# A Fourier-mixing layer beside a ReLU MLP on one Trainium2 core: the opening stretch re-ordered, twelve x tiles transposed by DMA

## Chip, core and metric

One NeuronCore of a Trainium2 chip. Five engines have queues of their own that run in order: PE (TensorE, matmuls and weight loads), DVE (VectorE), ACT (ScalarE), POOL (GpSimd) and SP (SyncE, which here only issues DMAs). Sixteen DMA engines move the data. Matmul results land in PSUM; everything else lives in SBUF or in HBM. The metric is the device time of one launch in microseconds (us); lower is better.

## What is computed

x is 2048 x 576, w1 576 x 4608, w2 4608 x 576, all float32.

```python
xn = _layernorm(x, axis=-1)
a = xn @ dft_hid_re.T ;  b = xn @ dft_hid_im.T
A = dft_seq_re @ a - dft_seq_im @ b
B = relu(xn @ w1) @ w2
return x + A + B
```

(The einsums of the reference are written as matrix products here.)

## The kernel before

**Arithmetic.** Each float32 operand is split into two float16 parts, `hi` and `lo`, after a scaling by a power of two, and each product is three float16 matmuls. Products on w2, and most others, are done as seven block products instead of eight (the `PRODUCTS` list, numbered 0 to 6), so that sums of blocks (`S1..S4` of the activations, `T1..T4` of w2) are built first, on DVE.

**Stages.** x is cut into 16 tiles of 128 rows and 4 groups of 4 tiles (tiles 0 to 3, 4 to 7, 8 to 11, 12 to 15). The hidden dimension of the MLP is cut into 9 blocks of 512 columns. A step is a pair (block, group): `mlp1` makes relu(xn w1) of it, `mlp1_out` evicts it from PSUM (ACT writes the hi parts, DVE the lo parts and the sums), and one step later `mlp2` multiplies it by w2. The 36 steps run from the start to about 815 us; the DFT along the hidden dimension and then the one along the sequence follow. The change touches the opening stretch (the first 62 us or so), and what it moves reaches to about 120 us.

**How a tile of x is made ready.** `stats` (L197) takes mean and variance of a group on DVE (`bn_stats`, `bn_aggr`), one square root on ACT (L215), and six small DVE instructions. `normalize` (N, L242) writes the normalised tile in float32 on DVE (L247) and its float16 high part on ACT (L249), into one of four staging buffers (`dbufs`, tile number modulo 4). `remainder` (E, L251) subtracts the two for the low part, on POOL in the opening stretch and on DVE later. Then the tile is transposed into `xT`: either by ten PE transposes into PSUM and two ACT copies out of it (`transposes`, T, L268; tiles 0 to 7), or by two DMA transposes on SP's queue (`transposes_dma`, TD, L260; tiles 8 to 15): nine blocks of 128 columns, and the last 128 columns once more for the half-filled block.

**The opening stretch** (L747 to L864) is written out by hand. Loads of x, w1 and w2 go out on SP, then sixteen copies of x from HBM to the HBM buffers `spill` (L760), to which POOL's accumulating DMAs (L573) later add the MLP's output. Four tiles of group 0 and then group 1 are transposed and multiplied by w1 block 0 (`tile_by`, then `mlp1` on whole groups). Meanwhile w2's scale is worked out: ACT sums magnitudes (`sum_w2`, L646), PE and DVE find the largest (`power_pe`, L152), and `split_w2` and `sums_w2` make the float16 parts. The steps of `prepare_w2(0)` are a list `w`: `w[0]`, `w[1]` sum magnitudes, `w[3]` makes the scale, `w[4]`/`w[6]` split the four plain blocks of the two halves, `w[5]`/`w[7]` make the sums, the rest split the sums. The stretch ends with products 0 to 2 on w2, the first two `mlp1` results of group 2 (`early`), and products 3 to 6.

**What sets the order.** A planner puts each engine's instructions into a queue: in program order where an instruction is ready by its own estimate of times, else behind others that are ready. `tc.issue_after(i)` (and `behind(key)`, which looks an instruction up in the dictionary `order`) makes what is traced inside it follow `i` on `i`'s own engine; on other engines it does nothing. Waits between engines are put in by the framework from the data.

**After the opening stretch** comes the loop over steps (L963). Its first pass, `n == 2`, does group 2 of block 0 and makes tiles 12 to 15 ready (N, E on DVE, TD). `work()` takes the next item of `todo`, which prepares the weights of the coming block: `load_w1`, `max_w1`, `split_w1`, `load_w2`, `sum_w2`, and so on; their raw loads share two buffers.

Of the kernel before, what the change touches and what calls it, by code (L numbers as in the profile page):

```python
# [49 lines left out]
def kernel(  # L50
# [47 lines left out]
    def load_raw(key, src, shape):  # L98
        r = raws[key] = raw.tile(shape, F32, tag="raw", name="raw_" + "_".join(map(str, key)))
        nc.sync.dma_start(r, src)  # L100
# [8 lines left out]
    def load_w2(b, i):  # L109
        load_raw(("w2", b, i), w2[b, i], [P, 4, EH])  # L110

# [40 lines left out]
    def power_pe(s, p, m):  # L152

        n = m.shape[-1]
        ps = ps2.tile([P, 2, 512], F32, tag="ps2", name="pm")

        for c in range(n):
            nc.tensor.matmul(
                ps[:1, 0, c * P : (c + 1) * P], m[:, c : c + 1], ident.bitcast(BF16),
                start=True, stop=True,  # L160
            )
        top = small.tile([1, n], BF16, tag=f"top{n}", name="top")
        nc.vector.tensor_reduce(
            top, ps[:1, 0, : n * P].rearrange("p (n f) -> p n f", f=P), AX.X, ALU.max
        )
        nc.tensor.matmul(ps[:, 1, :n], ones, top, start=True, stop=True)
        half = small.tile([P, n], F32, tag=f"half{n}", name="half")
        nc.vector.tensor_scalar(half, ps[:, 1, :n], 2.0**-107, 2.0**6, ALU.max, ALU.mult)
# [11 lines left out]
    def split(hi, lo, src, s):  # L180

        nc.scalar.activation(hi, src, AF.Copy, scale=s)  # L182
        nc.vector.scalar_tensor_tensor(lo, src, s, hi, ALU.mult, ALU.subtract)  # L183
# [13 lines left out]
    def stats(ts, after=None):  # L197
# [9 lines left out]
        for i, st in enumerate(sts):  # L207
            nc.vector.bn_aggr(mv[:, i], st.rearrange("p a b -> p (a b)"))
            yield
# [32 lines left out]
    def normalize(t, eng=nc.vector, after=None):  # L242
        stage = dbufs[t % 4]
        xn = xns[t] = stage[:, :D]

        xs = xss[t] = stage[:, D : 2 * D].bitcast(F16)
        eng.tensor_scalar(xn, acc[t], means[t], factors[t], ALU.subtract, ALU.mult)  # L247
        with behind(after):
            nc.scalar.activation(xs[:, :D], acc[t], AF.Identity, bias=shifts[t], scale=factors[t])  # L249

    def remainder(t, eng):  # L251
        xn, xs = xns[t], xss[t]
        eng.tensor_tensor(
            xs[:, D : D + REM], xn[:, KM * P :], xs[:, KM * P : D], ALU.subtract
        )
        eng.tensor_tensor(
            xs[:, D + REM :], xn[:, : KM * P], xs[:, : KM * P], ALU.subtract
        )

    def transposes_dma(t):  # L260

        xs = xss[t]
        g, c = divmod(t, TG)
        dst = xT[g][:, :, c * P : (c + 1) * P]
        nc.sync.dma_start_transpose(dst[:, :NKX], xs)
        nc.sync.dma_start_transpose(dst[:, NKX], xs[:, D - P : D])

    def transposes(t):  # L268
        xs = xss[t]
        pt = ps2.tile([P, 2, 1024], F16, tag="ps2", name=f"pt{t}")  # L270
        for k in range(NKX):
            nc.tensor.transpose(
                pt[:, k // 8, (k % 8) * P : (k % 8 + 1) * P], xs[:, k * P : (k + 1) * P], ident
            )
        g, c = divmod(t, TG)

        nc.tensor.transpose(pt[:, 1, P : 2 * P], xs[:, D - P : D], ident)
        dst = xT[g][:, :, c * P : (c + 1) * P]
        nc.scalar.activation(
            dst[:, :8, :], pt[:, 0, :].rearrange("p (k t) -> p k t", t=P), AF.Copy  # L280
        )
        order["xT", t] = nc.scalar.activation(
            dst[:, 8:, :], pt[:, 1, : 2 * P].rearrange("p (k t) -> p k t", t=P), AF.Copy
        ).ins
# [37 lines left out]
    def mlp1_group(b, g, i, cols, ps, wk=WK, start=True, stop=True):  # L322
        for n, (kx, hl, k) in enumerate(wk):
            nc.tensor.matmul(  # L324
                ps[:, cols], w1s[b, i // 2][:, hl, i % 2 * KT + k], xT[g][:, kx, cols],
                start=(start and n == 0), stop=(stop and n == len(wk) - 1),
            )
# [29 lines left out]
    def mlp1_out(b, g, i, pa, pb, after=None):  # L357
# [8 lines left out]
        for q, src in ((slice(A11, A11 + 1), a11), (slice(A12, A22 + 1), pb)):  # L366
            hi, lo = (h[:, n, q].rearrange("p a b -> p (a b)") for n in range(2))
            with behind(after):
                nc.scalar.activation(hi, src, AF.Relu)
            stt(lo, src, 0.0, hi, ALU.max, ALU.subtract)  # L370
        stt(s3, a11, 0.0, r21, ALU.max, ALU.subtract)
        stt(s1, a22, 0.0, r21, ALU.max, ALU.add)
        stt(s2, a22, 0.0, s3, ALU.max, ALU.subtract)
        stt(s4, a12, 0.0, s2, ALU.max, ALU.subtract)
# [167 lines left out]
    def mlp2(b, g, n):  # L542
# [25 lines left out]
        else:  # L568
            o = sums[row, col]
            add = nc.vector.scalar_tensor_tensor(o, ps, us[b], o, ALU.mult, ALU.add)  # L570
            order["acc"] = order["vfree"] = add.ins
        if n not in (0, 2, 3):
# [4 lines left out]
    def max_w1(b, f):  # L577
# [6 lines left out]
        with behind("vfree" if b >= BB else ("sh", 1) if f > 1 else None):  # L584
# [65 lines left out]
    def power_w2(b):  # L650
# [3 lines left out]
        else:  # L654
            m = small.tile([P, NQ], BF16, tag="mb2", name=f"mb2_{b}")
            with behind(("sh", 8)):
# [29 lines left out]
    def split_w2(b, i, c):  # L686
# [5 lines left out]
        with behind(None if b else ("xT", 7)):  # L692
            split(w[:, 0, q], w[:, 1, q], src, sc["w2", b][:, i : i + 1])
# [64 lines left out]
    for g, row, col in spill:  # L758
        src = x[(g * TG + row * 2) * P : (g * TG + row * 2 + 2) * P, col * EH : (col + 1) * EH]
        nc.sync.dma_start(spill[g, row, col], src.rearrange("(c p) e -> p c e", p=P))  # L760
# [12 lines left out]
    N, E, T, TD = normalize, remainder, transposes, transposes_dma  # L773
# [37 lines left out]
    T(2)  # L811
# [4 lines left out]
    tile_by(1, (3,), ps)  # L816
    T(3)
    weave(stats([4, 5, 6, 7]))
    N(4)
    E(4, GP)  # L820
# [14 lines left out]
    T(6)  # L835
    tile_by(5, (0, 1), qs)
    T(7)
    weave(stats([8, 9, 10, 11], ("sh", 4)))
    N(8, after=("xT", 5))
    E(8, GP)  # L840
    mlp1_out(0, 0, 1, *ps[2:], after=("xT", 6))
    for t in (9, 10, 11):
        N(t, after=("xT", 7))
        E(t, GP)
    tile_by(6, (0, 1), qs)
    w[3]()
    tile_by(7, (0, 1), qs)
    w[4]()
    w[5]()
    mlp1_out(0, 1, 0, *qs)  # L850
    for f in w[6:]:
        f()
    TD(8)
    q2 = [mlp1(0, 1, 2)]
    TD(9)
    q2.append(mlp1(0, 1, 3))
    mlp1_out(0, 1, 1, *q2)
    TD(10)
    TD(11)
# [85 lines left out]
    def first_c(m):  # L945
        n, q = divmod(m, 4)
        f = firsts[m] = mlp.tile([P, HK, P], F32, tag="first", name=f"f{n}_{q}", bufs=1)
        nc.sync.dma_start(f, blocks_c(n)[q])
# [14 lines left out]
    for n in range(2, len(steps)):  # L963
# [46 lines left out]
        for i in range(NF):  # L1010
# [4 lines left out]
            if i % 2:  # L1015
                mlp1_out(b, g, i // 2, *ps[i - 1 : i + 1])
# [3 lines left out]
            if n == 2:  # L1020
# [3 lines left out]
                transposes_dma(t)  # L1024
# [20 lines left out]
        if n == 2:  # L1045
            for q in range(7):
# [231 lines left out]
```

## Time and profile before

| | before |
|---|---|
| time, median of 3 runs | 1257.16 us (1255.46 to 1257.65) |
| time of the profiled execution | 1256.51 us |
| its span in the profile | 1254.7 us |
| PE busy | 1234.3 us (98%) |
| DVE busy | 1008.9 us (80%) |
| ACT busy | 704.8 us (56%) |
| POOL busy | 155.6 us (12%) |
| DMA moved | 158.08 MB, mean 126 GB/s |
| granted PE clock, mean | 0.999 |

The span runs from the first to the last profiled instruction; 1.8 us of the profiled execution's own time lie around it. A row of a timeline gives the start (us from the span's start), the duration, the engine and line, the operation, what is written and read, the number of instructions merged, and in brackets the engine's idle time before it and what ended it. Starts of successive instructions on one engine overlap by some 60 ns, so that start to start is the better price of one. A busy PE is not PE at its peak, so matmuls are best counted by the time from one start to the next.

### The profile page before, as it was taken

To read this page: it belongs to the slowest core of one execution; us is meant where nothing else is said; L and a number is where in the kernel's file an instruction comes from. 1 tells how busy PE (TensorE), PEld (TensorE's weight loads), DVE (VectorE), ACT (ScalarE), POOL (GpSimd) and SP (SyncE) were. 2 spreads that over 40 slices of the span, in tenths; PEclk is the share of its full clock that TensorE was granted. 3 is DMA by queue.
4 is the path that set the end of the run, shared out by engine and by line. 5 is a ranking of instruction groups with operands and counts; after the bars stand their busy time and mean duration, and the time that the engine had idled before them with its cause. 6 is when DMAs were issued, how large, how long until landed. Compare 5 with 4: busy or idle time off the path is not lost.

```text
span 1254.7 us, 25397 instructions
## 1 busy us (share of the span) xinstructions
PE 1234.3 (98%) x10309; PEld 983.5 (78%) x10309; DVE 1008.9 (80%) x1921; ACT 704.8 (56%) x1194; POOL 155.6 (12%) x199
## 2 busy tenths in 40 slices
PE   8799999999999999999999999999999999999998
PEld 7565657888888888888888888877777777777776
DVE  8999997878878778788787878566788878788885
ACT  5756566676666666766767666444453333333332
POOL 1321111212111111212121212100000000000000
PEclk9999999999999999999999999999999999999999
DMA  9576567666567665766576766630053434433420
GB/s 341 131 127 109 97 125 166 110 133 139 132 117 171 122 150 117 137 140 136 117 153 142 145 126 128 113 95 1 1 172 111 144 102 162 124 133 120 141 87 19
DMA packets 75909, 158.08 MB, mean 126 GB/s; under 512 B 17296, under 2 KB 36240, under 8 KB 75792
## 3 DMA queue, kind: packets, MB, share of 16 engines
q1 hardware_dynamic: 53008, 113.99, 28.3%
q0 software_dynamic: 22784, 42.48, 25.4%
q8 instruction: 80, 1.31, 0.4%
q14 instruction: 37, 0.30, 0.1%
HBM read 106.63 MB, written 51.90 MB: 126 GB/s over the span
## 4 chain that ended last, share of the span: by engine, by line
PE 74%; DVE 17%; DMA 4%; ACT 4%; issue 2%; POOL 0%; SPq 0%; DVEq 0%; ACTq 0%; POOLq 0%
PE p L1210 26%; PE p L556 19%; PE bank L479 19%; PE pd L1091 8%; DVE w2s L183 2%; DMA raw_w<-in_w_dram 1%; DMA acc<-in_x_dram 1%; DVE h L370 1%; PE p L324 1%; DVE h L501 1%; DVE h L377 1%; DMA f<-in_cre_dram 1%; ACT f L955 1%; DVE w1buf L183 1%; DVE dbuf L570 1%
## 5 line engine op out<-in xcount | busy, mean ns | idle before, releaser
L556 PE MATMUL p<-w2s,h 128*128 128x288 f16 x3024 | 409.8, 286 | 8.6 <-DVE w2s L183 3.3
L556 PEld LDWEIGHTS <-h 128*128 128x128 f16 x3024 | 295.5, 98 | 85.7 <-issue 9.8
L1210 PE MATMUL p<-R,cs 128*128 128x288 f16 x2688 | 329.4, 286 | 0.0
L1210 PEld LDWEIGHTS <-cs 128*128 128x128 f16 x2688 | 263.0, 98 | 66.3
L182 ACT ACTIVATE cs<-c,sc_c 128x1024 f16<-128x1024 f32 x112 | 125.1, 1144 | 196.8 <-DVE c L1153 72.6
L183 DVE SCALAR_TENSOR_TENSOR cs<-c,sc_c,cs 128x1024 f16<-128x1024 f32 x112 | 141.0, 1282 | 54.4 <-ACT cs L182 54.4
L479 PEld LDWEIGHTS <-w1buf 128*128 128x128 f16 x1600 | 156.5, 98 | 22.8 <-issue 1.7
L479 PEld LDWEIGHTS <-dbuf 128*128 128x128 f16 x1200 | 117.4, 98 | 17.5 <-issue 1.7
L479 PE MATMUL bank<-xT,w1buf 128*128 128x256 f16 x832 | 109.8, 273 | 0.0
L1091 PE MATMUL pd<-dbuf,xT 128*128 128x288 f16 x832 | 103.8, 286 | 0.0
L479 PE MATMUL bank<-acc,w1buf 128*128 128x256 f16 x768 | 102.1, 273 | 1.0 <-DVE acc L509 0.9
L1091 PEld LDWEIGHTS <-xT 128*128 128x128 f16 x832 | 80.8, 98 | 22.0 <-issue 1.9
L501 DVE TENSOR_TENSOR h<-s,h 128x1024 f16<-128x1024 f32 x56 | 68.5, 1223 | 33.9 <-ACT h L498 33.6
L573 POOL DMA_DIRECT2D spill<-dbuf x70 | 60.9, 875 | 233.1 <-DVE dbuf L570 201.9
L486 ACT ACTIVATE h<-acc 128x256 f16<-128x256 f32 x112 | 45.9, 411 | 77.5 <-DVE acc L509 74.8
L479 PE MATMUL bank<-xT,dbuf 128*128 128x256 f16 x624 | 82.4, 273 | 0.0
L498 ACT ACTIVATE h<-s 128x1024 f16<-128x1024 f32 x56 | 59.1, 1056 | 35.9 <-DVE s L493 35.1
L479 PE MATMUL bank<-acc,dbuf 128*128 128x256 f16 x576 | 76.6, 273 | 1.0 <-DVE acc L509 0.9
L1216 DVE SCALAR_TENSOR_TENSOR o<-p,us_c,o 128x288 f32<-128x288 f32 x112 | 57.5, 514 | 12.9 <-PE p L1210 12.3
L955 ACT ACTIVATE f<-f 128x1024 f32<-128x1024 f32 x64 | 66.9, 1046 | 0.6 <-DMA f<-in_cre_dram 0.6
L487 DVE SCALAR_TENSOR_TENSOR h<-acc,h 128x256 f16<-128x256 f32 x112 | 47.2, 422 | 21.0 <-ACT h L486 20.8
L573 POOL DMA_DIRECT2D spill<-sum x42 | 36.3, 865 | 184.9 <-DVE sum L570 159.8
(158 smaller groups left out, 1536.8 us busy)
## 6 DMA issues: line engine op xcount, KB each, us to landing
spill<-dbuf POOLq DMA_DIRECT2D x70, 288.0 KB, 5.2
f<-in_cre_dram SPq DMA_DIRECT2D x32, 512.0 KB, 5.8
f<-in_cim_dram SPq DMA_DIRECT2D x32, 512.0 KB, 5.2
c<-in_cre_dram SPq DMA_DIRECT2D x32, 512.0 KB, 4.1
c<-in_cim_dram SPq DMA_DIRECT2D x32, 512.0 KB, 5.0
spill<-sum POOLq DMA_DIRECT2D x42, 288.0 KB, 4.6
raw_w<-in_w_dram SPq DMA_DIRECT2D x17, 640.0 KB, 6.0
raw_w<-in_w_dram SPq DMA_DIRECT2D x18, 576.0 KB, 4.9
```

Source lines behind the costliest of these rows:

```text
L182: nc.scalar.activation(hi, src, AF.Copy, scale=s)
L183: nc.vector.scalar_tensor_tensor(lo, src, s, hi, ALU.mult, ALU.subtract)
L479: nc.tensor.matmul(ps, l, r, start=first and m == 0, stop=m == len(todo) - 1, skip_group_check=not first,)
L487: stt(lo, src, 0.0, hi, ALU.max, ALU.subtract)
L498: order["s"] = nc.scalar.activation(hi_s, st[:, 1:], AF.Copy).ins
L501: order["lo"] = nc.vector.tensor_tensor(lo_s, st[:, 1:], hi_s, ALU.subtract).ins
L556: order["pe"] = nc.tensor.matmul(ps[:, c], h[:, x, qa, c * P : (c + 1) * P], w[:, y, qb], start=first and i == 0 and j == 0, stop=i == NQ ...
L573: nc.gpsimd.dma_start(spill[g, row, col], o, accum_op=ALU.add)
L955: nc.scalar.activation(f, f, AF.Abs, scale=2.0**-10, accum_out=sums_c[:, n, q : q + 1])
L1091: nc.tensor.matmul(ps[j], xT[g][:, kx, c * P : (c + 1) * P], dsp[j][:, hl, k], start=(t % 2 == 0 and n == 0), stop=(t % 2 == 1 and n == le ...
L1210: nc.tensor.matmul(ps, w[:, a, k], r[:, c, rq], start=first and k == 0 and j == 0, stop=k == HK - 1 and j == 2, skip_group_check=not first,)
L1216: order["o"] = nc.vector.scalar_tensor_tensor(o, ps, us["c"][:, n : n + 1], o, ALU.mult, ALU.add).ins
```

## The change

Tiles 0 to 3 are still transposed on PE; tiles 4 to 7 now go by DMA as 8 to 15 did, and every DMA tile takes one DMA of ten blocks instead of two: the staging buffer is 64 float32 columns longer, and an extra instruction (POOL for tiles 4 to 11, ACT for 12 to 15) first copies the last 128 columns behind the low part. The copies of x to `spill` leave the start of SP's queue: group 0's follow tile 11's DMA, group 1's follow tile 15's, and those of groups 2 and 3 follow the first and second load of block 1's w2. The statistics of tiles 8 to 11, N(7) and w2's scale come ahead of the first eviction; the normalised float32 parts of tiles 10 and 11 go from DVE to ACT; both plain splits of w2 come before any of its sums; and product 0 on w2 comes ahead of the first two results of group 2, products 1 to 6 behind them.

```diff
     def load_raw(key, src, shape):
-        nc.sync.dma_start(r, src)
+        order["raw"] = nc.sync.dma_start(r, src).ins
     def load_w2(b, i):
         load_raw(("w2", b, i), w2[b, i], [P, 4, EH])
+        if b == 1:
+            copy_x(2 + i, "raw")
...
-        xs = xss[t] = stage[:, D : 2 * D].bitcast(F16)
-        eng.tensor_scalar(xn, acc[t], means[t], factors[t], ALU.subtract, ALU.mult)
+        xs = xss[t] = stage[:, D : 2 * D + P // 2].bitcast(F16)
         with behind(after):
+            if eng is nc.scalar:
+                nc.scalar.activation(xn, acc[t], AF.Identity, bias=shifts[t], scale=factors[t])
+            else:
+                eng.tensor_scalar(xn, acc[t], means[t], factors[t], ALU.subtract, ALU.mult)
             nc.scalar.activation(xs[:, :D], acc[t], AF.Identity, bias=shifts[t], scale=factors[t])
...
-        dst = xT[g][:, :, c * P : (c + 1) * P]
-        nc.sync.dma_start_transpose(dst[:, :NKX], xs)
-        nc.sync.dma_start_transpose(dst[:, NKX], xs[:, D - P : D])
+        again = xs[:, 2 * D :], xs[:, D - P : D]
+        if eng is nc.scalar:
+            eng.activation(*again, AF.Copy)
+        else:
+            eng.tensor_copy(*again)
+        with behind("td"):
+            order["td"] = nc.sync.dma_start_transpose(xT[g][:, :, c * P : (c + 1) * P], xs).ins
...
-    for g, row, col in spill:
-        src = x[...]
-        nc.sync.dma_start(spill[g, row, col], src.rearrange("(c p) e -> p c e", p=P))
+    def copy_x(g, key="td"):
+        for row, col in itertools.product(range(2), range(2)):
+            t = g * TG + row * 2
+            src = x[t * P : (t + 2) * P, col * EH : (col + 1) * EH]
+            with behind(key):
+                nc.sync.dma_start(spill[g, row, col], src.rearrange("(c p) e -> p c e", p=P))
...
+    weave(stats([4, 5, 6, 7]))
+    copies(2, pt, ("root", 4))
     T(3)
-    weave(stats([4, 5, 6, 7]))
-    N(4)
-    E(4, GP)
     w = prepare_w2(0)
     w[0]()
     w[1]()
     tile_by(2, (0, 1, 2, 3), ps)
-    for t in (5, 6, 7):
+    for t in (4, 5, 6):
         N(t)
         E(t, GP)
-    T(4)
+        TD(t, GP)
     tile_by(3, (0, 1, 2, 3), ps)
+    weave(stats([8, 9, 10, 11], ("sh", 4)))
+    N(7, after=("root", 8))
+    E(7, GP)
+    TD(7, GP)
+    w[3]()
     pq = ps2.tile([P, 2, 512], F32, tag="ps2", name="p1_0_1")
     qs = [pq[:, 0], pq[:, 1]]
-    T(5)
-    tile_by(4, (0, 1), qs)
-    mlp1_out(0, 0, 0, *ps[:2])
...
+    mlp1_out(0, 0, 0, *ps[:2], after="top")
+    order["s0"] = order["s"]
+    with behind("pm"):
+        for t in (4, 5):
+            tile_by(t, (0, 1), qs)
+    for t in (8, 9):
+        N(t, after="s4")
         E(t, GP)
+        TD(t, GP)
+    mlp1_out(0, 0, 1, *ps[2:])
+    for t in (6, 7):
+        tile_by(t, (0, 1), qs)
+    for t in (10, 11):
+        N(t, nc.scalar, after="s0")
+        E(t, GP)
+        TD(t, GP)
     w[4]()
+    w[6]()
+    mlp1_out(0, 1, 0, *qs)
+    q2 = [mlp1(0, 1, 2), mlp1(0, 1, 3)]
     w[5]()
-    mlp1_out(0, 1, 0, *qs)
-    for f in w[6:]:
+    for f in w[7:]:
         f()
...
-    for q in range(3):
-        mlp2(0, 0, q)
-    with tc.issue_after(order["pe"]):
+    mlp1_out(0, 1, 1, *q2, after="w2")
+    copy_x(0)
+    mlp2(0, 0, 0)
+    with behind("pe"):
         early = [mlp1(0, 2, 0), mlp1(0, 2, 1)]
-    for q in range(3, 7):
+    with behind("m1"):
+        mlp2(0, 0, 1)
+    for q in range(2, 7):
         mlp2(0, 0, q)
...
-                transposes_dma(t)
+                transposes_dma(t, nc.scalar)
...
         if n == 2:
+            copy_x(1)
             for q in range(7):
                 mlp2(pb, pg, q)
```

The rest of the diff hands out names for the `behind` anchors ("top" and "pm" in `power_pe`, "hi" and "s4" in `mlp1_out`, "w2hi" and "w2" in `split_w2`, "m1", "add", "stats"), puts the DVE instructions of an eviction behind the same anchor as the ACT ones, and parts `transposes` into its PE half and `copies`.

More of the change, by code (lines that the diff above doesn't have):

```diff
@@ L274, in transposes, with copies @@
             )
+        nc.tensor.transpose(pt[:, 1, P : 2 * P], xs[:, D - P : D], ident)
+        return pt
+    def copies(t, pt, after=None):
         g, c = divmod(t, TG)
-        nc.tensor.transpose(pt[:, 1, P : 2 * P], xs[:, D - P : D], ident)
         dst = xT[g][:, :, c * P : (c + 1) * P]
[L279 to L284, printed above, removed]
+        with behind(after):
+            nc.scalar.activation(
+                dst[:, :8, :], pt[:, 0, :].rearrange("p (k t) -> p k t", t=P), AF.Copy
+            )
+            nc.scalar.activation(
+                dst[:, 8:, :], pt[:, 1, : 2 * P].rearrange("p (k t) -> p k t", t=P), AF.Copy
+            )
     A11, A12, A22, S1, S2, S3, S4 = range(7)
```

75 lines of the change are left out of this document (31 added, 44 removed).

## The prediction, made before the changed kernel was run

> **What bounds the kernel now.** I read the sums of long stretches first, then the timelines of PE and DVE at the places where one waits. In a row of sums stand the stretch and its length, the busy time of PE, PE's weight loads, DVE, ACT and POOL with their instructions, the granted PE clock, the DMA engines' share and GB/s.
>
> ```profile
> 24.00:49.90 25.90, 24.11 (x329) 19.46 (x330) 21.25 (x61) 22.51 (x40) 12.88 (x18) 1.00 0.76 202
> 49.90:62.10 12.20, 5.99 (x37) 3.60 (x36) 12.20 (x23) 6.31 (x9) 0.00 (x0) 0.96 0.36 90
> 62.10:187.50 125.40, 123.74 (x775) 74.37 (x774) 119.11 (x251) 73.17 (x121) 26.72 (x29) 0.99 0.65 116
> 187.50:1254.70 1067.20, 1060.87 (x8935) 869.01 (x8934) 835.62 (x1508) 591.86 (x1009) 112.81 (x144) 1.00 0.52 121
> ```
>
> Four regimes. After 187.5 us PE is full (1060.87 of 1067.20) and DVE has room: what is won before that point is kept, and nothing is won behind it. From 49.9 to 62.1 PE waits and DVE is full without a break. From 62.1 to 187.5 both are full, PE with 1.7 us to spare and DVE with 6.3. So time that PE gains before 62 only reaches the end if DVE gets as far ahead. Does PE really lean on DVE in that third stretch? Its only three named waits say yes:
>
> ```profile
> 117.98 2.50 PE L556 MATMUL p<-w2s,h 128*128 128x288 f16 x19 [0.35 <-DVE h L370]
> 158.54 1.63 PE L556 MATMUL p<-w2s,h 128*128 128x288 f16 x12 [0.52 <-DVE dbuf L570]
> 187.48 1.63 PE L556 MATMUL p<-w2s,h 128*128 128x288 f16 x12 [0.58 <-ACT dbuf L567]
> ```
>
> They are short, but each is a point where PE and the DVE/ACT side meet with no slack. I therefore price the change on DVE, and treat PE's own saving as an upper case.
>
> **The change, part by part.** *PE in the opening.* Four tiles of ten transposes go.
>
> ```profile
> 36.05 0.67 PE L272 MATMUL pt<-ident,dbuf 128*128 128x128 f16 x9
> ...
> 36.61 1.73 PE L324 MATMUL p<-xT,w1buf 128*128 128x128 f16 x28
> ...
> 59.80 0.28 PE L556 MATMUL p<-w2s,h 128*128 128x288 f16 x1 [1.87 <-ACT w2s L182]
> ...
> 62.10 7.42 PE L324 MATMUL p<-xT,w1buf 128*128 128x512 f16 x28
> 69.36 6.04 PE L556 MATMUL p<-w2s,h 128*128 128x288 f16 x48
> 75.24 6.21 PE L324 MATMUL p<-xT,w1buf 128*128 128x512 f16 x28
> ```
>
> Start to start a tile's transposes take 36.61 - 36.05 = 0.56 us, four take 2.2. Products 0 to 2 on w2 are 36 matmuls; 48 take 75.24 - 69.36 = 5.88, so 36 need 4.4 of the 12.2 us before 62.1: 7.8 us of stall. The change puts 28 matmuls of group 2 (6.2 us) into it. They also ran slow, 7.42 against 6.21: 1.2 us of low clock after the thin stretch. PE's possible saving is 2.2 + 7.8 + 1.2 = 11.2 us, plus up to 1.8 idle before 49.9 (25.90 - 24.11), less a new pause at `pm` (below).
>
> The clock, row first:
>
> ```profile
> 62.00:62.50 0.50, 0.50 (x3) 0.16 (x2) 0.50 (x2) 0.15 (x1) 0.00 (x0) 0.50 0.88 266
> ```
>
> It fell to 0.50 although the longest single wait was 1.87 us. The Trainium skill (TensorE: Matmul & The Clock Gate, "HAM oscillation — how this bites in real kernels") asks for no PE gap over about 3.4 us; by that rule this stretch would not have lost its clock and PE's saving would be 1.2 us smaller. The row decides, and the rule's gap is too generous here.
>
> *DVE in the opening*, which decides:
>
> ```profile
> 25.91 0.18 DVE L216 RECIPROCAL r<-u 128x4 f32<-128x4 f32 x1 [2.06 <-ACT u L215]
> ...
> 27.00 2.04 DVE L247 TENSOR_SCALAR dbuf<-acc,mv,r 128x576 f32<-128x576 f32 x4
> ...
> 34.13 0.42 DVE L370 SCALAR_TENSOR_TENSOR h<-p,h 128x256 f16<-128x256 f32 x1 [1.87 <-ACT h L369]
> ...
> 40.48 1.13 DVE L657 CAST mb<-c_mw 128x2 bf16<-128x2 f32 x1
> ...
> 44.61 0.16 DVE L168 TENSOR_SCALAR half<-pm 128x2 f32<-128x2 f32 x1 [0.43 <-PE pm L166]
> ...
> 45.83 1.05 DVE L661 TENSOR_TENSOR c_pp<-c_pw,c_pw 128x2 f32<-128x2 f32 x1
> ```
> ```profile
> 24.40 1.02 ACT L279 ACTIVATE xT<-pt 128x1024 f16<-128x1024 f16 x1 [1.28 <-PE pt L277]
> ...
> 25.58 0.30 ACT L215 ACTIVATE u<-mv,eps 128x4 f32<-128x4 f32 x1
> ```
>
> (a) DVE waited 2.06 us for the square root, which stood behind tile 2's copies on ACT. ACT was idle before them, so with the copies behind the root only the root itself and its hand-over are left, some 0.35: -1.7 (bounds -2.06 and -1.2). The copies start no more than 0.3 later.
> (b) The 1.87 wait before the first eviction: ACT loses four tiles' copies, while DVE's part now follows `top`. The chain cast, `pm`, `top` must end first; I let half remain, -1.0 (bounds -1.87 and 0).
> (c) Two of the float32 parts go to ACT: 2.04 / 4 = 0.51 each, -1.0. ACT pays two L249-like instructions and loses copies that cost more (L279 alone is 1.02 a tile).
> (d) The 0.43 wait for `pm` goes, as the scale is made while other work is there: -0.4 (bounds -0.43 and 0.5).
> (e) Small instructions that were stretched: the cast took 1.13 and `c_pp` 1.05 where instructions on two columns beside them take 0.16. They ran beside POOL, the last to its very end:
>
> ```profile
> 29.04 0.30 POOL L253 TENSOR_TENSOR dbuf<-dbuf 128x64 f16<-128x64 f32 x1 [3.81 <-DVE dbuf L247]
> ...
> 45.71 1.15 POOL L256 TENSOR_TENSOR dbuf<-dbuf 128x512 f16<-128x512 f32 x1
> ```
>
> POOL now does eight tiles with hardly a break, so they stay stretched: 0 (bounds -1.9, both cured, and +1.9, two more hit). The Trainium skill (Advanced Engine Details and Errata, "Mode Summary") says that the second Vector SBUF port is shared with GpSimd and that the two block each other; it speaks against the eight added POOL copies. The rows agree (POOL's instruction ends at 45.71 + 1.15 = 46.86, `c_pp` at 46.88); by the rule alone (e) would be a loss of up to one POOL instruction for each such DVE instruction.
>
> DVE's head start is then -1.7 - 1.0 - 1.0 - 0.4 = -4.1 us.
>
> *`pm` on PE.* Tiles 4 to 7's matmuls queue behind the second `pm` matmul, and the third eviction waits for them.
>
> ```profile
> 41.67 0.27 PE L158 MATMUL pm<-ident,mb 128*1 128x128 bf16 x2 [0.56 <-DVE mb L657]
> ...
> 44.41 0.17 PE L166 MATMUL pm<-top,ones 1*128 1x2 bf16 x1
> ```
>
> PE pauses between 0.5 us and the 2.7 seen here (44.41 - 41.67). For the end I take nothing: DVE then has two evictions, N(8), N(9) and two splits in front of it. Without that cover it would be the pause itself.
>
> *The twelve tiles by DMA.*
>
> ```profile
> 49.45 1.31 SPq L265 DMA_TRANSPOSE xT<-dbuf  x1
> 50.81 1.23 SPq L266 DMA_TRANSPOSE xT<-dbuf  x1
> ```
> ```profile
> xT<-dbuf SPq DMA_TRANSPOSE x16, 3.4
> ```
>
> Nine blocks cost SP 1.31, one block 1.23; ten should cost about 1.31 x 10/9 = 1.5 (bounds 1.31 and 2.54), so a tile saves SP about 1.1. The extra copy lies on POOL between 0.30 (64 columns) and 1.15 (512); nearer the first, 0.4. POOL then needs 0.30 + 1.15 + 0.4 = 1.85 us a tile. It began tile 4 at 29.04; from there tile 7 is done at 36.4 and lands 3.4 later, near 40, and tile 11, without a break, at 43.8 + 3.4, near 47. PE would want group 1 at about 40 and group 2 at about 48 (40, the 6.2 us of 28 matmuls, 1.5 of product 0): just in time. Landings 2 us later would cost PE, not DVE, so 0 for the end. On tiles 12 to 15 the copy is on ACT, which is busy 73.17 of 125.40: 0.
>
> *The copies of x and w2's loads.*
>
> ```profile
> 18.07 12.77 SPq L760 DMA_DIRECT2D spill<-in_x_dram  x16
> ```
> ```profile
> spill<-in_x_dram SPq DMA_DIRECT2D x16, 288.0 KB, 6.9
> ...
> raw_w<-in_w_dram SPq DMA_DIRECT2D x18, 576.0 KB, 4.9
> ```
> ```profile
> 90.00:100.00 10.00, 10.00 (x67) 5.91 (x65) 9.90 (x20) 6.49 (x11) 3.35 (x4) 1.00 1.04 204
> 100.00:110.00 10.00, 10.00 (x69) 6.57 (x68) 9.15 (x23) 6.28 (x10) 1.37 (x2) 1.00 0.26 36
> ```
> ```profile
> 101.21 1.16 ACT L646 ACTIVATE j<-raw_w 128x1152 f32<-128x1152 f32 x1 [1.23 <-DMA raw_w<-in_w_dram]
> ```
> ```profile
> q0 software_dynamic: 845, 0.91, 69.1%
> ```
> ```profile
> 88.44 7.67 SPq L100 DMA_DIRECT2D raw_w<-in_w_dram  x2
> ```
> ```profile
> 99.92 1.09 POOL L573 DMA_DIRECT2D spill<-acc  x1 [5.37 <-DVE acc L570]
> 102.64 0.36 POOL L121 PARTITION_ALL_REDUCE top<-c_mw  x1 [1.63 <-ACT j L646]
> ```
>
> At the start the copies lay beside nothing that matters. A group's four now take 4 x 12.77 / 16 = 3.2 us, and groups 1 and 2 go out just ahead of w2's second load, in a stretch whose DMA share is 1.04. That load is awaited: ACT stood 1.23 us for it, then POOL and DVE. On POOL's queue the all-reduce at 102.64 stands behind a spill that must now wait for group 2's copies. (f) A DMA behind a full queue lands in 6.9 rather than 4.9: +2.0 (bounds 0, and two groups of copies in front, +6.4). Group 0's copies fall behind tile 11, ahead of any spill, and group 3's into the stretch with share 0.26: 0.
>
> *Later DVE waits.*
>
> ```profile
> 72.58 0.82 DVE L570 SCALAR_TENSOR_TENSOR acc<-p,c_ub,acc 128x576 f32<-128x576 f32 x1 [1.16 <-ACT dbuf L249]
> ```
>
> (g) This adds up a product on w2 that PE was only just finishing (L249 had its turn on ACT). With PE far ahead it goes: -1.2 (bounds -1.2 and 0). Splits ahead of sums, and the other anchors, move the same instructions within a full queue: 0.
>
> Sum: -4.1 + 2.0 - 1.2 = -3.3 us. The profiled execution took 1256.51 (the span and 1.8 around it), 0.65 below the median of 1257.16: 1256.51 - 3.3 = **1253.2 us**.
>
> **The rivals.** *PE's saving comes through.* If DVE's order bends with PE (evictions ahead of weight preparation), the limit is DVE's whole idle time, 4.1 + 6.3 = 10.4, just under PE's 11.2: 1246.1. For it: ten of PE's microseconds are real stalls. Against it: the three meetings above, and program order puts weight work ahead of evictions.
> *Swallowed.* DVE's start is kept, but the meeting at 187.48, where PE waited for ACT and not for DVE, or a late w2 load, holds the old time: gain under 1 us, 1256. For it: ACT's instructions there stand in an order that the change leaves alone. The case that the change does not do what it says belongs here: if POOL and SP bring tile 11 as late as before (52), PE still stalls, and only the DVE terms are left.
> *Slower: DMA.* One mechanism, at 86 to 105 us: groups 1 and 2 of the copies, 6.4 us, stand in front of w2's second load, the second group's spills wait for their copies and then run beside it (half of what they took of the DMA engines from 90 to 100, 69.1% of 10 us: 3.4), and ACT's L646, POOL's all-reduce and DVE behind it stand for 9.8. Less 4.1 + 1.2 that makes +4.5: 1261.0. It decides once the load is more than 5.3 us later than its trigger asks. For it: the share over 1. Against: the two loads' issues lay 7.3 us apart (88.44 to 88.44 + 7.67 less one issue), time in which copies drain.
>
> **How the numbers follow.** Forecast 0.50, own range 1249 to 1256 (terms a to g at their bounds, not all at once); PE's saving 0.18; swallowed 0.17; slower 0.15. Runs of this kernel tell apart about 0.2%, 2.5 us: 0.9 of the forecast lies beyond that, with the first rival 0.63 faster; the rest of the forecast and the swallowed case 0.22 within; 0.15 slower. The range takes in the first rival and half of the way to the last: 1245.0 to 1259.5.
>
> **What would show it.** In the opening: the wait of DVE for L215 under 0.5; no stall over 1 us on PE between product 0 and product 6; no half clock near 62. Right if PE comes out of group 2's last two results (81.3 before, 75.24 + 6.21 less the overlap) some 10 us earlier while the step at 117.98 comes only 4 to 6 earlier, with longer PE waits for DVE in between. Wrong if PE's lead is still 9 us at 187 (first rival), or if ACT's L646 waits several us for w2's second load (last rival). A tile DMA that takes over 2.5 us of SP, or lands later than 5 us, would undo the tile part.

## The result, and the profile after

The changed kernel takes **1260.29 us** (median of 7 runs, 1259.82 to 1262.50); the kernel before takes 1256.51 on the same chip. The ratio is 1.0032, interval 1.0021 to 1.0044: **slower by some 4 us**, where 3 us of gain were forecast. The profiled execution took 1260.05, its span is 1258.3.

The sums of the four stretches first, columns as in the prediction:

```profile
24.00:49.90 25.90, 22.86 (x296) 19.01 (x293) 25.43 (x61) 20.38 (x36) 18.50 (x25) 0.93 0.53 90
49.90:62.10 12.20, 10.29 (x64) 5.95 (x62) 11.80 (x24) 6.58 (x10) 0.66 (x1) 1.00 0.80 230
62.10:187.50 125.40, 114.12 (x719) 69.16 (x718) 114.41 (x239) 69.61 (x119) 25.89 (x29) 0.99 0.68 140
187.50:1258.30 1070.80, 1064.74 (x8960) 871.38 (x8958) 838.50 (x1518) 594.64 (x1012) 112.80 (x145) 1.00 0.52 121
```

The second row is what the change is made for: PE works 10.29 of the 12.20 us in which it had worked 5.99. The third row takes it back: PE idles 125.40 - 114.12 = 11.3 us there, against 1.7 before, and DVE 11.0 against 6.3. Behind 187.5 us nothing is lost: PE idles 6.1 us there and 6.3 before. Two slices of the third stretch show where the time goes:

```profile
90.00:100.00 10.00, 10.00 (x69) 6.11 (x67) 8.10 (x15) 5.49 (x10) 4.36 (x4) 1.00 1.13 280
100.00:110.00 10.00, 6.53 (x33) 3.66 (x31) 4.19 (x13) 3.91 (x7) 0.36 (x1) 0.83 0.79 204
```

From 100 to 110 us PE works 6.53 of 10 us and DVE 4.19 (10.00 and 9.15 before), after a slice in which the DMA share was 1.13. Rows of the timelines of SP's queue, ACT, POOL and DVE name what they stand for:

```profile
81.72 2.64 SPq L782 DMA_DIRECT2D spill<-in_x_dram  x4
84.41 0.60 SPq L977 DMA_DIRECT2D f<-in_cre_dram  x1
85.31 0.34 SPq L100 DMA_DIRECT2D raw_w<-in_w_dram  x1
85.69 4.05 SPq L782 DMA_DIRECT2D spill<-in_x_dram  x4
93.07 0.33 SPq L100 DMA_DIRECT2D raw_w<-in_w_dram  x1
```
```profile
103.98 1.16 ACT L663 ACTIVATE j<-raw_w 128x1152 f32<-128x1152 f32 x1 [7.57 <-DMA raw_w<-in_w_dram]
```
```profile
89.98 3.30 POOL L590 DMA_DIRECT2D spill<-acc  x3 [3.02 <-DMA spill<-in_x_dram]
...
105.41 0.36 POOL L123 PARTITION_ALL_REDUCE top<-c_mw  x1 [8.34 <-ACT j L663]
```
```profile
105.81 0.17 DVE L126 TENSOR_SCALAR half<-top 128x2 f32<-128x2 f32 x1 [7.64 <-POOL top L123]
```

Read as one chain: w2's second load is issued at 93.07 and ACT can use it at 103.98, **10.9 us** from issue to use. Before, it was issued at 88.44 + 7.67 - 0.3 = 95.8 and used at 101.21: 5.4 us. In front of it on SP's queue lie group 1's four copies, the f load (a 512 KB block of the sequence matrix, of which the prediction says nothing), w2's first load and group 2's four copies. From the view of the copies' line (L782), 85.6 to 90 us, what group 2's four took:

```profile
DMA to landing us min/median/max: 9.1/10.7/12.6
```

The last was issued at 89.06, so it lands at 101.7, 8.6 us behind the second load's issue. POOL's three accumulating spills waited 3.02 us for group 1's copies and then ran beside the load. ACT stands for 7.57 us, POOL's all-reduce behind ACT, DVE for 7.64 behind POOL. Before, DVE's wait at this place was short:

```profile
103.03 0.17 DVE L124 TENSOR_SCALAR half<-top 128x2 f32<-128x2 f32 x1 [0.82 <-POOL top L121]
```

PE's timeline gives the account of the lead. First the kernel before at three places that the prediction does not quote, then the kernel after:

```profile
97.70 0.61 PE L349 MATMUL p<-xT,w1buf 64*128 64x512 f16 x4
...
112.58 1.63 PE L556 MATMUL p<-w2s,h 128*128 128x288 f16 x12
...
205.36 1.69 PE L479 MATMUL bank<-xT,w1buf 128*128 128x256 f16 x14
```
```profile
35.16 0.16 PE L168 MATMUL pm<-top,ones 1*128 1x2 bf16 x1 [2.90 <-DVE top L165]
...
52.59 6.20 PE L339 MATMUL p<-xT,w1buf 128*128 128x512 f16 x28 [1.91 <-DMA xT<-dbuf]
...
67.44 6.21 PE L339 MATMUL p<-xT,w1buf 128*128 128x512 f16 x28
...
83.82 0.38 PE L339 MATMUL p<-xT,w1buf 128*128 128x512 f16 x1 [2.62 <-DVE dbuf L452]
...
94.19 0.60 PE L364 MATMUL p<-xT,w1buf 64*128 64x512 f16 x4
...
106.92 4.52 PE L572 MATMUL p<-w2s,h 128*128 128x288 f16 x24 [3.47 <-ACT acc L583]
...
115.25 1.63 PE L572 MATMUL p<-w2s,h 128*128 128x288 f16 x12 [1.00 <-DVE acc L586]
...
181.49 1.63 PE L572 MATMUL p<-w2s,h 128*128 128x288 f16 x12 [1.64 <-ACT sum L583]
...
209.38 1.69 PE L495 MATMUL bank<-xT,w1buf 128*128 128x256 f16 x14
```

The same work stands at 75.24 before and 67.44 after, **7.8 us ahead**. At 97.70 against 94.19 the lead is **3.5**: PE has met the DVE and ACT side again, waiting for tile 15 and for evictions. (The row at 83.82 names a DVE instruction, but tile 15's DMA, issued at 80.32, landed 3.4 us later, just ahead of it.) At 112.58 against 115.25 it is **2.7 behind**: w2's late load took 6.2. Of that, 1.4 us are low clock behind the pause: 24 matmuls take 4.52 us at 106.92 where others take 3.10, with a granted clock of 0.83 in that slice. At 205.36 against 209.38 it is **4.0 behind**: 1.3 more went on the way, mostly at the wait for ACT at 181.49. The medians differ by 3.8.

### The profile page after: what moved, and what is told of

Read it like the earlier page. It is cut to its first block, busy times and chain, and to the rows that moved or that the text cites. A ratio compares the mean times of both kernels' runs of the same rounds, so it can differ in the third digit from the quotient of the medians.

```text
span 1258.3 us, 25304 instructions
## 1 busy us (share of the span) xinstructions
PE 1231.6 (98%) x10269; PEld 983.0 (78%) x10269; DVE 1011.0 (80%) x1919; ACT 702.4 (56%) x1192; POOL 161.2 (13%) x207
## 4 chain that ended last, share of the span: by engine, by line
PE 78%; DVE 12%; ACT 1%; issue 1%; DMA 1%; POOL 0%; DVEq 0%; POOLq 0%; ACTq 0%
PE p L1240 26%; PE p L572 22%; PE bank L495 21%; PE pd L1121 8%; DVE w2s L186 2%; DMA raw_w<-in_w_dram 1%; PE p L339 1%; DVE dbuf L456 1%; DVE h L517 1%; DVE h L385 1%; DVE acc L441 1%; ACT w2s L185 0%; DVE sum L586 0%; DVE raw_w L697 0%; DVE dbuf L586 0%
```

## The experiments

The theory is that the transfers moved ahead of w2's second load turned a small gain into a loss (the queue). Its rival is that the gain of the opening is swallowed later on the DVE and ACT side, whatever the transfers do. Letters in an expectation mean what that expectation says of them. The kernel before was run beside each batch: medians 1256.83 (first four experiments), 1256.63 (next four), 1256.43 (last four). Ratios are to those. In experiments 1 to 5, 9, 11 and 12 the instructions of PE, DVE, ACT and POOL run in the order of the kernel that was edited; only SP's order of DMAs differs. In 6 to 8 and 10 the planner made a new order for other engines as well, which is said there.

**1. Copies of group 1 and later ahead of tile 12.**

```diff
+            order["w1"] = nc.sync.dma_start(...).ins
+        if b == 1 and i == 1:
+            copy_x(2, "w1")
+            copy_x(3, "w1")
...
-        if b == 1:
-            copy_x(2 + i, "raw")
...
     copy_x(0)
+    copy_x(1)
...
-            copy_x(1)
```

> The changed kernel with the copies of x for group 1 put behind group 0's, and those of groups 2 and 3 behind block 1's loads of w1, all ahead of tile 12's transpose; nothing else. Theory Q (queue: copies stand in front of w2's second load, which in the changed kernel landed 10.83 us after its issue against 5.34 before, and ACT stood 7.57 us for it): the load lands in 5 to 6 us, ACT's wait on L663 falls under 2 us, PE's 3.47 us wait and the slow matmuls behind it go, and the time falls by 5 to 7 us, to about 1253 to 1255. Theory O (the order of the instructions on DVE, ACT, POOL and PE is what costs, the copies are beside the point): the load lands sooner but the time moves by less than 1.5 us, 1259 to 1261.

1257.92 us, ratio 1.0010 (1.0001 to 1.0018): 2.4 us better than the change, but no gain, and between what the two theories said. w2's second load came 5.4 us after its issue, as before the change. But now eight copies stand in front of block 1's w1 loads, and DVE waited for those, as it did not in the changed kernel (the profiled execution took 1260.36, the longest of twelve):

```profile
63.83 0.82 DVE L118 TENSOR_REDUCE c_mf<-raw_w 128x1 f32<-128x640 f32 x1 [3.08 <-DMA raw_w<-in_w_dram]
```

So part of the queue's cost was moved to another awaited load.

**2. The kernel before, with nothing but the copies moved.**

```diff
-    for g, row, col in spill:
-        nc.sync.dma_start(spill[g, row, col], ...)
+    copy_x(0)
...
+            copy_x(1)
...
+        if b == 1:
+            copy_x(2 + i, "raw")
```

> The kernel before with only the copies of x moved to the places they have in the changed kernel (group 0 behind tile 11, group 1 behind tile 15, groups 2 and 3 behind w2's first and second load); transposes and order as before. Theory Q: w2's second load lands about 10 us after its issue, ACT waits about 6 us for it instead of 1.23, and the kernel is slower by 4 to 6 us, 1260.5 to 1262.5. Theory O: within 1 us of the kernel before, 1255.5 to 1257.5.

1259.79 us, ratio 1.0027 (1.0017 to 1.0037). The moved copies alone cost the old kernel some 3 us, though there ACT stood for the load by only 1.6 us more than before:

```profile
105.08 1.16 ACT L648 ACTIVATE j<-raw_w 128x1152 f32<-128x1152 f32 x1 [2.84 <-DMA raw_w<-in_w_dram]
```

It came at 105.08 against 101.21: group 1's copies lie among the DMAs of tiles 13 to 15 there, and PE waited 1.12 us for one of these too. So the place of the copies does harm without any other part of the change. The size is less than the queue theory's 4 to 6 us, and ACT's wait less than its 6; the f load stays early in this kernel.

**3. The f load early; 4. groups 2 and 3 behind w2's second load; 5. both.**

```diff
-        with tc.issue_after(order["td"]):
-            nc.sync.dma_start(f, blocks_c(n)[q])
+        nc.sync.dma_start(f, blocks_c(n)[q])
```
```diff
-        if b == 1:
-            copy_x(2 + i, "raw")
+        if b == 1 and i == 1:
+            copy_x(2, "raw")
+            copy_x(3, "raw")
```

> The changed kernel with one edit undone: the first block of the sequence matrix (512 KB) is loaded as early as the queue lets it, not behind tile 15's transpose. Theory Q: 512 KB less in front of w2's loads; at 288 KB in some 0.8 us that is 1.4 us, so ACT's wait falls from 7.57 to about 6 and the time by 1 to 1.5 us, to about 1259. Theory O: no change, 1260 to 1261.

> The changed kernel with group 2's copies behind w2's second load instead of its first (group 3's behind them). Theory Q in its plain form: 3.2 us of copies less in front of the second load, which lands about 7.5 us after its issue; time lower by 2 to 3.5 us, about 1257. Theory Q with POOL's queue as the gate: group 2's first spill then waits longer for its copies and the all-reduce of w2's maxima stands behind it on POOL, so DVE's wait on L126 stays at 7 us or grows and nothing is won, 1260 to 1262. Theory O: no change.

> The changed kernel with the two helpful edits together: the first block of the sequence matrix loaded early, and group 2's copies behind w2's second load. Theory Q: in front of the second load are left group 1's copies alone; it lands 5 to 6 us after its issue, ACT's wait on L663 (7.57 changed, 3.2 and 3.9 with one edit each) falls to about 1 to 2.5, and the time to about 1254 to 1255.5. Theory S (the load is no longer what is late last: what the opening won on DVE is too little, and the waits for tiles 11 and 15 and for ACT's evictions hold the rest): the wait falls as said but the time stays at 1256 to 1257, as with one edit alone.

Experiments 3 and 4, ACT's row of the second load:

```profile
101.10 1.16 ACT L663 ACTIVATE j<-raw_w 128x1152 f32<-128x1152 f32 x1 [3.19 <-DMA raw_w<-in_w_dram]
```
```profile
100.11 1.16 ACT L664 ACTIVATE j<-raw_w 128x1152 f32<-128x1152 f32 x1 [3.88 <-DMA raw_w<-in_w_dram]
```

| | time | ratio (interval) | ACT's wait for the load | DVE's wait |
|---|---|---|---|---|
| change | 1260.29 | 1.0032 (1.0021 to 1.0044) | 7.57 | 7.64 |
| f early | 1256.90 | 1.0004 (0.9996 to 1.0013) | 3.19 | 3.26 |
| groups 2, 3 behind | 1256.56 | 1.0000 (0.9991 to 1.0009) | 3.88 | 3.95 |
| both | 1256.50 | 0.9996 (0.9987 to 1.0006) | 3.28 | 3.36 |

Either edit alone gives back the whole loss, 3.4 and 3.7 us; the second adds nothing that can be told. For the loss the queue is shown: two edits that touch nothing but the order of SP's DMAs remove it. The first was expected to be worth 1 to 1.5 us, so the gain is not simply the load's own share of the queue. The form of the theory in which POOL's queue is the gate fell: with group 2's copies behind the load, DVE's wait shrank to 3.95. That the two edits don't add up says that something else then sets the time: with both, ACT's wait did not fall to the 1 to 2.5 expected, and the time is that of the rival in the expectation. With both, group 1's copies (81.8 to 84.4) still go out ahead of w2's first load, group 1's spills wait for them and then run beside the second load, which ACT gets 99.74 - 93.1 = 6.6 us after its issue. Experiment 9 takes that up.

**6 to 8. Copies of groups 0 to 2 at the start; the extra copies on ACT; the extra copies twice.** Groups 0 to 2 go out right behind the loads of x, group 3 behind w2's second load, and the f load is early. Experiment 7 also hands the extra copies of tiles 4 to 11 to ACT (four calls), 8 makes POOL do each of them twice.

```diff
+    for g in range(3):
+        copy_x(g)
```

> The changed kernel with no copies near w2's loads: groups 0 to 2 right behind the loads of x (where all sixteen copies stood before), group 3 behind w2's second load, the sequence matrix's first block early. From 20 to 30 us the changed kernel used the DMA engines to 0.14 only, so they should fit there, with tile 4's transpose late by 1 us at most. Theory Q: ACT's wait for w2's second load under 1 us; with the head start on DVE that the changed kernel's opening shows (DVE's eviction of the last results of group 1 ends at 62.9 with one magnitude less done, 65.2 before: some 1.6 us) the time is 1253.5 to 1255.5. Theory P (prediction's sizes for DVE were right, 4.1 us and 1.2 later): 1250.5 to 1252. Theory S: 1256 to 1257.

> e6 with the extra 128-column copies of tiles 4 to 11 on ACT instead of POOL; nothing else. Theory C (contention: in the changed kernel DVE's instructions from 24 to 63 us ran 5.6 us over their shortest forms, 2.4 before, where they lay beside POOL's, so POOL's eight extra instructions took DVE's head start away): the stretch falls by 1 us or more and the time by 0.5 to 1.5 us against e6. Rival: POOL's remainders alone stretch DVE; no change, or ACT's added 2 us make the tiles later and the time 0.5 to 1 us longer.

> e6 with POOL doing each of those eight copies twice (2.3 us more on POOL at 0.28 each); the second writes the same data again. Theory C: DVE is stretched by another 1 to 2 us and the time is longer than e6 by 0.5 to 2 us; tiles 7 and 11 land 1.1 us later, which by itself costs PE and not DVE. Rival: no change within 0.5 us.

1260.71, 1260.29 and 1261.93 us: ratios 1.0034 (1.0022 to 1.0045), 1.0030 (1.0018 to 1.0043) and 1.0043 (1.0027 to 1.0058). Experiment 6 is as slow as the change, though no copies stand in front of w2's second load any more and ACT does not wait for it, and 7 and 8 cannot be told from it. They are no clean test of where the copies stand: with other DMAs in front, the planner ordered DVE's queue anew. In experiment 6 (the profiled execution took 1258.05, the shortest of six) the second half of w2's split starts at 48.51, where the changed kernel runs both halves together at 43.65. Tile 11 then comes late, and the accumulating spills of group 0 go out in a bunch beside the DMAs of tiles 13 to 15, so that these take far longer:

```profile
55.00 7.90 PE L339 MATMUL p<-xT,w1buf 128*128 128x512 f16 x28 [4.17 <-DMA xT<-dbuf]
```
```profile
DMA to landing us min/median/max: 3.4/7.6/9.9
```

(The second fence is from the view of the transposing DMA's line, 70 to 95 us; alone such a DMA lands in 3.4.) What the copies at the start would do in an unchanged order was not found out. The contention theory of 7 and 8 fails all the same: DVE's stretch, counted as in experiment 10 below, is 6.7 us in 6, 7.2 with the copies off POOL and 5.6 with twice as many on it, and 8 keeps the order that 6 has on DVE and ACT. The three say one thing: a transfer's place also decides an order elsewhere.

**9. Group 1's copies behind block 1's w1 loads**, on top of experiment 5.

```diff
+            order["w1"] = nc.sync.dma_start(...).ins
+        if b == 1 and i == 1:
+            copy_x(1, "w1")
...
-            copy_x(1)
```

> The changed kernel with the f load early, groups 2 and 3 of the copies behind w2's second load, and now group 1's copies behind block 1's w1 loads (issued near 57 us), where DMA has room until 66. Theory T (the loss is the queue ahead of w2's second load): the load lands in at most 5.6 us, near 98, DVE's wait behind POOL's all-reduce falls from 3.4 to under 1 us, and the time comes to 1253.5 to 1255. Rival S (what is left of the lead meets the DVE and ACT side at 111 to 178 us anyway): the load lands early as well, but the waits move to products on w2 there and the time stays at 1256 to 1257.

```profile
101.83 0.17 DVE L129 TENSOR_SCALAR half<-top 128x2 f32<-128x2 f32 x1 [2.20 <-POOL top L126]
```

1255.26 us, ratio 0.9992 (0.9984 to 1.0001), the lowest of the kernels that compute all of the reference. ACT gets the load 5.5 us after its issue, as the queue theory has it, but DVE still waits 2.20, not under 1: it arrives there early. The time lies between the two theories. The version beats the changed kernel by 5 us; that it beats the kernel before by 1.2 is likely but not shown, as the interval just reaches 1.

**10. The extra copies of tiles 4 to 11 on ACT**, on top of experiment 5.

```diff
-        TD(t, GP)
+        TD(t, nc.scalar)
```

> The kernel with f early and groups 2 and 3 behind w2's second load, and the extra copies of tiles 4 to 11 on ACT in place of POOL. Theory P (the added POOL copies stretch DVE's small instructions): what DVE's instructions from 24 to 63 us take over the shortest of their form falls from 6.4 to near 3, and DVE reaches the sums of group 1's second result 2 to 3 us earlier. Rival O (the stretch belongs to POOL's remainders, which both kernels have, and to where DVE's order now puts its small instructions): it stays over 5.5, and the time within 1 us of 1256.5.

1256.51 us, ratio 1.0002 (0.9994 to 1.0011). Summed over DVE's instructions from 24 to 63 us, the time above the shortest of the same form in all these kernels is 3.1 us in the kernel before, 6.4 in the changed one and in experiment 5, and 7.0 here (the expectation of experiment 7 has 2.4 and 5.6 for the first two). That the added POOL copies stretch DVE's instructions (P) is refuted: without any copy on POOL the stretch is still there. From 35 us on DVE's order is another one here, but up to there it is the same, and the stretch is 4.0 against 3.3 in experiment 5. DVE's timeline, then POOL's:

```profile
32.94 1.08 DVE L228 TENSOR_SCALAR u<-u 128x4 f32<-128x4 f32 x1
```
```profile
32.85 1.15 POOL L264 TENSOR_TENSOR dbuf<-dbuf 128x512 f16<-128x512 f32 x1
```

The stretched instruction starts just behind a remainder of POOL's (L264) and ends with it, within 0.03 us. These remainders are in both kernels.

**11 and 12. No copies of x at all**, in the changed kernel with the f load early (11), and in the kernel before (12), where the loop of copies is left out. Both leave x and most spilled sums out of the result.

```diff
     def copy_x(g, key="td"):
+        return
...
-            nc.gpsimd.dma_start(spill[g, row, col], o, accum_op=ALU.add)
+            nc.gpsimd.dma_start(spill[g, row, col], o)
```

> The changed kernel with the f load early, without any copy of x: the spills write their sums instead of adding to them, so x and all but the last spilled sum of each part are missing from the output. To be read beside the kernel before with the same left out (e12). Theory T: with nothing moved in front of w2's second load, the change's other parts keep a gain of 2 to 4 us over e12. Rival S: e11 and e12 are within 1 us of one another, so that the head start of the opening is lost on the DVE and ACT side whatever the transfers do.

> The kernel before without any copy of x, spills written and not added: the output lacks x and all but the last spilled sum of each part. In the kernel before the copies lay at 17 to 31 us, where DMA was awaited by nobody, so under both theories the time is 1255 to 1257, with w2's second load near its 5.3 us or a little under.

1252.86 us (1251.30 to 1253.52) and 1254.58 us (1254.30 to 1255.75). Their runs do not overlap: with no copies about, the rest of the change **gains 1.7 us** by the medians (2.1 by the means), about the lower end of the first theory's 2 to 4, and more than the rival's 1. Experiment 12 itself came out under the 1255 to 1257 expected: leaving out the copies and the adding is worth 1.9 us in the kernel before too. DVE's wait for w2's second load and PE's one late wait, of experiment 11:

```profile
99.61 0.17 DVE L127 TENSOR_SCALAR half<-top 128x2 f32<-128x2 f32 x1 [0.29 <-POOL top L124]
```
```profile
139.66 0.61 PE L365 MATMUL p<-xT,dbuf 64*128 64x512 f16 x4
...
161.82 0.60 PE L365 MATMUL p<-xT,dbuf 64*128 64x512 f16 x4
...
174.22 1.63 PE L573 MATMUL p<-w2s,h 128*128 128x288 f16 x12 [1.64 <-ACT sum L584]
...
203.65 1.63 PE L573 MATMUL p<-w2s,h 128*128 128x288 f16 x12
```

and PE in experiment 12:

```profile
142.97 0.61 PE L349 MATMUL p<-xT,dbuf 64*128 64x512 f16 x4
...
165.12 0.60 PE L349 MATMUL p<-xT,dbuf 64*128 64x512 f16 x4
...
186.58 1.63 PE L556 MATMUL p<-w2s,h 128*128 128x288 f16 x12 [0.52 <-ACT dbuf L567]
...
205.99 1.63 PE L556 MATMUL p<-w2s,h 128*128 128x288 f16 x12
```

With the load no longer late, the lead of 3.3 us (139.66 against 142.97) holds to 161.82 against 165.12, and 1.0 of it is lost at the wait for ACT: 203.65 against 205.99 leaves 2.3. That is the rival's share, about a third. Plain spills are also lighter than accumulating ones (issuing one holds POOL for 0.69 us in experiment 11 and 1.08 in the changed kernel), so that these two kernels say what the opening is worth, not what a kernel with its copies could reach.

## Why the prediction was wrong

Its frame held, and so did most terms for DVE. One term, (f), was far too small; wide DVE instructions beside POOL had no term at all; and the case that came true was the last rival, with the sign that the text named for it: ACT waits 7.57 us for w2's second load.

**The step that failed: (f), the copies in front of w2's second load.** The text gave +2.0 us, bounds 0 and 6.4: a landing in 6.9 in place of 4.9, as behind a full queue; and against the last rival it held that copies drain in the 7.3 us between the two loads' issues. They did not drain in time: group 2's copies landed up to 8.6 us behind the second load's issue. In front of them lay a 512 KB load of f, which neither the account of the change nor the part on w2's loads mentions: the diff puts it behind tile 15's DMA (`first_c`), where the kernel before issued it at 41.77. The spills held back by the copies came on top. Issue to use went from 5.4 to 10.9 us, and PE from 3.5 ahead to 2.7 behind, so (f) is **+6.2**, almost the upper bound. Without any copies the lead stays: in experiment 11 against 12, 3.3 us of it still stand at 140. Experiments 3 and 4 show that the cost is no sum of parts: take away either the f load or group 2's copies and 3.4 to 3.7 us come back. One path that the text gave for (f) was not taken: the all-reduce did not stand behind a spill that waits for group 2's copies (that spill, at 96.00, waited for DVE alone) but behind ACT, for 8.34 us. The forecast's other choice here, group 0's copies behind tile 11 at nothing, is not refuted for the changed kernel, but experiment 1 shows how near the next awaited load is.

**Term (e), DVE instructions beside POOL.** Taken as 0, bounds ±1.9, for small instructions alone; over all of DVE's instructions it came to +3.3 (6.4 against 3.1). Two rows of DVE and one of POOL before, then DVE and POOL after:

```profile
36.71 0.16 DVE L221 TENSOR_TENSOR u<-u,r 128x4 f32<-128x4 f32 x1
...
37.88 1.22 DVE L377 TENSOR_TENSOR h<-s,h 128x1024 f16<-128x1024 f32 x1
```
```profile
39.71 0.53 POOL L253 TENSOR_TENSOR dbuf<-dbuf 128x64 f16<-128x64 f32 x1 [4.59 <-PE pt L277]
```
```profile
32.10 1.07 DVE L225 TENSOR_TENSOR u<-u,r 128x4 f32<-128x4 f32 x1
...
39.57 2.12 DVE L393 TENSOR_TENSOR h<-s,h 128x1024 f16<-128x1024 f32 x1
```
```profile
32.00 1.15 POOL L263 TENSOR_TENSOR dbuf<-dbuf 128x512 f16<-128x512 f32 x1
...
39.44 1.16 POOL L263 TENSOR_TENSOR dbuf<-dbuf 128x512 f16<-128x512 f32 x1
40.56 1.28 POOL L260 TENSOR_TENSOR dbuf<-dbuf 128x64 f16<-128x64 f32 x1
```

For the small instructions (up to four columns) the 0 was nearly right: their stretch went from 2.5 to 3.1 us. The cast, `c_tw` and `c_pp`, stretched by 2.3 together, are cured, and three instructions of the `stats` chains, now among POOL's remainders, are stretched by 2.5. The six behind the square root of tiles 8 to 11 ran in a pause of POOL's before (4.59 us, up to 39.71); now two of them each wait a remainder out, the first shown here: 32.00 + 1.15 = 33.15, and 32.10 + 1.07 = 33.17. What no term had is the rest, 0.6 before and 3.3 after: wide instructions. The subtraction for the lo sums (L377, now L393) ran in the same pause before, in 1.22; at 39.57 it starts behind a remainder, takes 2.12, and POOL's next instruction takes 1.28 where others of its shape take 0.30. Four such instructions make 2.6 us. The prediction looked for the cause in the added copies; experiment 10 shows that these are not needed for it. That it is the moved instructions is read from the rows, and was not tried by itself. The Trainium skill (SBUF — State Buffer, "Who interferes with whom") says that a DVE instruction with two SBUF inputs contends with a GpSimd instruction that reads SBUF, and that the first to issue keeps the shared port pair to its end; these rows agree, with 0.16 us become 1.07. (The sentence of the Trainium skill that the prediction cites for the shared port, from Advanced Engine Details and Errata, "Mode Summary", is said there of 2p Vector instructions; the section named first is the one that covers a tensor_tensor such as `c_pp`.) Its list could have been held against each moved DVE instruction beforehand.

**What was right.** (a) DVE's wait for the root fell from 2.06 to 0.36, as given. (b) and (d): both waits went altogether, a little more than the 1.0 and 0.4 assumed. With (c), taken as forecast, the four make -1.7 - 1.9 - 1.0 - 0.4 = -5.0, and with +3.3 for (e) -1.7. DVE reaches the lo sums of group 1's second result (L377, now L393) at 61.76 against 64.06, with one magnitude of 0.7 us less done: 1.6 ahead, where 4.1 were forecast. (g) The wait of 1.16 us at 72.58 is gone as well. The half clock near 62 went as said, and of PE's stalls there one is left, 1.91 us at 52.59 for tile 11: the prediction had it landing near 47, it was transposed by 52.5, since POOL took up tiles 8 to 11 with pauses and was itself stretched (one L263 took 2.13 us where others take 1.15). That cost lead that DVE could not have followed. The DMAs themselves were priced well: the one of tile 15 takes SP 1.35 us, and the median of the twelve lands in 3.5.

`pm` held PE for 2.90 us (35.16), a little over its bound, and cost the end nothing that can be seen.

**The rivals.** "PE's saving comes through" fell as the text argued: 7.8 us of lead shrank to 3.5 before w2's load was met. "Swallowed" has a part: the wait for ACT's sum late in the third stretch is 1.64 us in the changed kernel and in experiment 11, 0.58 and 0.52 in the kernels without the change, and costs about 1 us. "Slower: DMA" gave 1261.0 and named place and mechanism; its price was made of other numbers (9.8 late less 5.3, against 6.2 less 3.5 and 1.3 lost later), so that it comes within 1 us of the measured time is in part luck. What stood against it, the drain of the copies, was argued and not worked out: four copies of 288 KB, a load of 512, one of 576, four copies more and the four spills of group 1 are 4.7 MB, the second load itself 0.6 more. At the 273 GB/s that the DMA engines moved from 81.7 to 103.9 us that is, as an estimate, 19 us of work from 81.7 on, to about 101; ACT had the load at 103.98.

## What to carry to other kernels

Moving a transfer "off the start" moves it in front of something: list what is issued behind it until the next awaited load, with every other transfer that the same edit carries along or that waits for the moved ones, and divide the bytes by the rate of that stretch. A DVE instruction moved into a stretch where POOL works cost up to one POOL instruction here, whether small (0.16 became 1.07) or wide (1.22 became 2.12). And a lead won on one engine is worth only what the others can follow: of 7.8 us on PE, 3.5 were left 27 us later.

## What was not expected of the hardware

A pause of PE of the same length did not always cost the clock. From 35 to 37 us, behind the wait for `pm`, 2.90 us in the changed kernel (above) and as long in experiment 9,

```profile
35.33 0.16 PE L171 MATMUL pm<-top,ones 1*128 1x2 bf16 x1 [2.90 <-DVE top L168]
```

the first and then the second had

```profile
35.00:37.00 2.00, 1.70 (x16) 1.55 (x16) 2.00 (x9) 1.14 (x2) 1.84 (x4) 0.50 1.12 211
```
```profile
35.00:37.00 2.00, 1.59 (x27) 1.44 (x27) 2.00 (x7) 1.14 (x2) 2.00 (x5) 1.00 1.10 211
```

a granted clock of 0.50 and of 1.00, with 16 and 27 matmuls done. Of the eight traces with a pause of 2.90 or 2.91 us here, the clock fell to 0.50 behind it in six and stayed at 1.00 in two (experiments 4 and 9). The Trainium skill (TensorE: Matmul & The Clock Gate, "What's actually happening") calls the activity window free-running and, for a kernel's start, the count of slow matmuls run-variable; the rows agree. A forecast of 1 us that hangs on the clock here cannot be made from the length of the pause.
